# A pre-LN block with linear attention and a gated FFN: a new order for the second half of the loop over k

## The chip, the cores and the metric

One core of a Trainium2 chip runs the whole program. The core has engines that run side by side, each with its own queue of instructions in a fixed order: TensorE (PE, matmuls and the weight loads that go with them), VectorE (DVE), ScalarE (ACT), GpSimd (POOL), and SyncE (SP), which here only issues DMAs. Engines wait for each other by semaphores. The metric is the device time of one execution in microseconds (us), of which the median counts.

## The reference

The input x has 2048 rows of 640. LN is a layer norm without gain.

```python
h  = x + attention(LN(x))
h2 = h + (gelu(LN(h) @ w_gate) * (LN(h) @ w_up)) @ w_down      # 640 -> 1536 -> 640
```

Attention is linear, with 32 heads of 20 columns. q, k and v are x's LN times the three parts of wqkv. With a head's w_phi (20 x 20), the features of q and k are two softmaxes, of q w_phi and of its negative, side by side (40 features). Per head, kv = features(k)^T v (40 x 20) and z = the column sums of features(k) over all rows. The output is features(q) kv / (features(q) z + 1e-6), then a product with wo.

## The kernel before, in words

Rows are split in 16 tiles t of 128, and these in four blocks of 512. All code runs under a schedule written out by hand: after line 663 the kernel is one list of calls such as `vm(12)`, and each engine executes its instructions in the order of that list. Nothing reorders them, so the list is the whole schedule; SP's DMAs stand in it too.

PSUM is cut into four equal buffers, which `gtile` hands out in turn and `give` returns. Every matmul product takes one until another engine has read it out.

The first half of the list loads x and weights, normalises rows and transposes them into LN1T. Per tile t, the loop over k does this:

- `ap(t, e)` normalises the rows on ACT ("a") or DVE ("v"), after `bn`, `rt` and `mr` on DVE and POOL; `dt(t)` transposes them by a DMA from SP into LN1T.
- `vm(t)` (L328) is the product for v, `ve(t)` copies it on ACT into vS. vS has eight buffers, for t modulo 8.
- `fm(i, d)` (L354) multiplies a part of W_q (i = 0) or W_k by the block-diagonal w_phi, `fc` copies it out. So `km(t)` (L375) is the product for k w_phi, and `ke(t, s)` (L382) its exponential on ACT, for s = 0 and its negative for s = 1, into E (eight buffers).
- `ks(t)` (L391) sums E per head on DVE, `kr(t)` (L395) takes the reciprocal into rs (three buffers), `kx(t, s, e)` (L401) multiplies v by it into vt, on DVE ("v") or POOL ("g"). So the softmax's division is put on v.
- `kv(t)` (L416) is called a visit here: 40 small matmuls (32 columns of E against 42 or 63 of vt) that add tile t's k^T v into kvp, which keeps one of the four PSUM buffers from the first visit to the last. The visits may come in any order of t.

`kv_clear` (POOL) builds a mask in parts, and `kv_mask` (DVE, L426 and L429) turns kvp into KV with it, after the last visit.

`qm(j)` (L444) is the product for q w_phi of one or two chunks of 128 columns for a block of 512 rows, `qe(j, s)` (L448) its exponentials on ACT. Then comes attention per tile: `ab` (L489, PE), `ae` (copy out of PSUM), `a_den`, `a_rec`, `a_w`, `a_o` (division and sum, DVE or POOL), a transpose by PE (`o_tr`, `o_tc`) or DMA (`o_dt`), `po_` (L544, the product with W_o), `res` (the residual). LN of h is `ap2` with `tr2` and `tc2`, or `dt2`. The FFN is `gu` (L617, gate and up products for one of 12 chunks of 128 columns), `gl` (gelu, ACT, L623), `gm` (product, DVE, L630) and `dn` (L642, the product with W_down). `gu(0, ...)` is the first FFN block. `gu` asks for all of W_gate and W_up, `po_` for all of W_o.

`load_w(name, c0, c1)` (L171) loads a part of W_o ("o"), W_gate ("g"), W_up ("u") or W_down ("d"). W_down's tile is taken in `ffn_pools()`, in memory that E and vt have used, so its loads wait for the last visit. SP issues its DMAs in order, and one that waits holds up those behind it.

Of the kernel before, what the change touches and what calls it, by code (L numbers as in the profile page):

```python
# [9 lines left out]
F32 = mybir.dt.float32  # L10
# [7 lines left out]
def kernel(  # L18
# [13 lines left out]
    P = 128  # L32
# [62 lines left out]
    def eq_tiles(pool, j0, j1):  # L95
# [9 lines left out]
    epsd = const.tile([P, 1], F32, name="epsd")  # L105
    eq_tiles(const, 0, 13)

    mid = ctx.enter_context(tc.tile_pool(name="mid", bufs=1, side="right"))
    LN1T = [mid.tile([P, NC, 512], BF16, name=f"LN1T{b}") for b in range(NB)]
    Wq2 = mid.tile([P, NC, D], BF16, name="Wq2")  # L110
# [3 lines left out]
    Wk2 = p1.tile([P, NC, D], BF16, name="Wk2")  # L114
    vS = [p1.tile([P, H, VC], BF16, name=f"vS{i}") for i in range(8)]
    WqT = p1.tile([P, NC, D], BF16, name="WqT")
    tsum, tsq, tlog, nrstd, prstd, tmean, trstd = (
        p1.tile([P, 4], F32, name=n) for n in ("tsum", "tsq", "tlog", "nrstd", "prstd", "tmean", "trstd"))
    fp_cm = tc.tile_pool(name="fp", bufs=1, side="right", reuse_waits="tile")
    fp = fp_cm.__enter__()  # L120
    WkT = fp.tile([P, NC, D], BF16, name="WkT")
# [141 lines left out]
    def rt(t, n, e):  # L263
        need(*(("bn", t + j) for j in range(n)))
        m = mv[t][0]
        ve, rstd = small(p1, [P, n], "ve1"), small(p1, [P, n], "rstd1")
        if e == "a":
            nc.scalar.activation(ve, m[:, :, 1], ACTF.Ln, bias=eps)
            nc.scalar.activation(rstd, ve, ACTF.Exp, scale=-0.5)
        else:  # L270
            nc.gpsimd.tensor_scalar_add(ve, m[:, :, 1], EPS)
            nc.gpsimd.tensor_tensor(rstd, ve, nhalf[:, 0:n], op=ALU.pow)
        for j in range(n):
            lnp[t + j] = [m[:, j, 0:1], rstd[:, j:j + 1], None]

    def mr(t):
        mean, rstd, _ = lnp[t]
        lnp[t][2] = small(p1, [P, 1], "mr1")
        nc.gpsimd.tensor_scalar(lnp[t][2], mean, rstd, -1.0, op0=ALU.mult, op1=ALU.mult)
# [42 lines left out]
    def vm(t, c0=0, c1=NC, by_chunk=True):  # L322
        need(*(("lnT", t, c) for c in range(c0, c1)), *(("Wv", c) for c in range(c0, c1)))
        if c0 == 0:
            pv[t] = gtile("pv")
        order = [(c, u) for c in range(c0, c1) for u in range(2)]
        for c, u in order if by_chunk else sorted(order, key=lambda x: x[1]):
            nc.tensor.matmul(pv[t][:, u, 0:HD], lhsT=lnT(t, c), rhs=Wv[:, c, u * HD:(u + 1) * HD],  # L328
                             start=(c == 0), stop=(c == NC - 1))
        if c1 == NC:  # L330
            have.add(("pv", t))

    def ve(t):
        need(("pv", t), *([("prstd", t)] if t in CT else []))
        nc.scalar.activation(vS[t % 8][:, :, 0:Dh].rearrange("p (u h) f -> p u h f", u=2),
                             pv[t][:, :, 0:HD].rearrange("p u (h f) -> p u h f", f=Dh), ACTF.Copy,
                             scale=col(prstd, t) if t in CT else 1.0)
        give(pv.pop(t))
        have.add(("v", t))
# [39 lines left out]
    def ke(t, s):  # L379
        if t not in Ek:  # L380
            Ek[t] = ev.tile([P, 2, D], BF16, name="E", bufs=EB)
        nc.scalar.activation(halves(Ek[t][:, s, :]), pk[t][:, :, 0:HD], ACTF.Exp,  # L382
                             scale=((col(prstd, t), col(nrstd, t)) if t in CT else (1.0, -1.0))[s])
        have.add(("ke", t, s))
        if ("ke", t, 1 - s) in have:
            give(pk.pop(t))

    def ks(t):
        need(("ke", t, 0), ("ke", t, 1))
        sk[t] = small(p1, [P, 2 * H], "sk")  # L390
        nc.vector.reduce_sum(sk[t], Ek[t].rearrange("p s (h f) -> p (s h) f", f=Dh), axis=AX.X)  # L391

    def kr(t):
        rs[t] = small(p1, [P, 2 * H], "rs")
        nc.vector.reciprocal(rs[t], sk.pop(t))  # L395

    def kx(t, s, e):
        need(("v", t))
        if t not in Vt:
            Vt[t] = ev.tile([P, 2, H, VC], BF16, name="vt", bufs=EB)  # L400
        E[e].tensor_tensor(Vt[t][:, s], vS[t % 8], rs[t][:, s * H:(s + 1) * H, None].to_broadcast([P, H, VC]), ALU.mult)  # L401
        have.add(("vt", t, s))
# [3 lines left out]
    def kv(t):  # L406
        need(("vt", t, 0), ("vt", t, 1))
        first, last = not kvn, len(kvn) == NT - 1
        if first:
            kvp.append(gtile("kvp"))  # L410
        kvn.append(t)
        for s in range(2):
            for c in range(NC):
                for g, r in enumerate(QT):
                    f0, h0 = 160 * g + 32 * c, 8 * g + HS[c]
                    nc.tensor.matmul(kvp[0][r, s, HO[c] * VC:(HO[c] + HW[c]) * VC], lhsT=Ek[t][:, s, f0:f0 + 32],  # L416
                                     rhs=Vt[t][:, s, h0:h0 + HW[c], :], start=(c == 0 and first),
                                     stop=last, skip_group_check=True)
        if last:
            have.add("kv")  # L420
# [477 lines left out]
    ap(11, "a")  # L898
    dt(11)
    kr(5)  # L900
    kx(5, 1, "g")
    bn(14, 1, 2)
    rt(14, 2, "g")
    kx(5, 0, "g")
    mr(14)
    kx(4, 0, "v")
    ks(6)
    kr(6)
    kx(6, 0, "g")
    mr(15)  # L910
    kx(6, 1, "v")
    ke(8, 0)
    vm(10, by_chunk=False)
    kv(3)
    ve(10)
    ks(8)
    km(10)
    ke(10, 1)
    fm(0, 0)
    fc(0, 0, "a")  # L920
    ke(10, 0)
    kv(4)
    kv(2)
    km(12)
    ke(12, 0)
    ke(12, 1)
    ks(7)
    ap(1, "v")
    kr(7)
    kx(7, 0, "g")  # L930
    kx(7, 1, "g")
    ks(9)
    kr(9)
    kr(8)
    kx(8, 0, "g")
    ap(2, "v")
    ap(14, "a")
    load_w("o", 0, 2)
    load_w("o", 2, 5)
    dt(14)  # L940
    vm(12, by_chunk=False)
    vm(11, by_chunk=False)
    ve(11)
    ve(12)
    km(13)
    ke(13, 1)
    fm(0, 2)
    fc(0, 2, "a")
    ks(12)
    kr(12)  # L950
    kx(12, 0, "v")
    ks(10)
    kx(9, 0, "g")
    kx(8, 1, "g")
    kx(9, 1, "g")
    kx(12, 1, "g")
    vm(13, by_chunk=False)
    kv(5)
    kv(6)
    kv(7)  # L960
    ke(13, 0)
    ks(13)
    kr(13)
    ve(13)
    ap(15, "a")
    vm(14, by_chunk=False)
    ve(14)
    fm(0, 4)
    fc(0, 4, "a")
    km(14)  # L970
    fm(0, 1)
    fc(0, 1, "a")
    ke(14, 1)
    km(11)
    ke(11, 1)
    ke(14, 0)
    ke(11, 0)
    dt(1)
    dt(2)
    qm(0)  # L980
    qe(0, 1)
    qe(0, 0)
    dt(15)
    vm(15, by_chunk=False)
    ve(15)
    km(15)
    ke(15, 0)
    qm(3)
    qe(3, 1)
    qe(3, 0)  # L990
    ke(15, 1)
    qm(1)
    qe(1, 1)
    qe(1, 0)
    kr(10)
    kx(10, 0, "g")
    kx(13, 0, "g")
    kx(10, 1, "g")
    kv(8)
    kv(10)  # L1000
    kv(12)
    kx(13, 1, "v")
    ks(14)
    kr(14)
    kx(14, 1, "g")
    kv(13)
    ks(11)
    kx(14, 0, "v")
    qm(2)
    qe(2, 1)  # L1010
    qe(2, 0)
    kr(11)
    kx(11, 0, "g")
    kx(11, 1, "g")
    kv(11)
    ks(15)
    kr(15)
    kx(15, 0, "v")
    kx(15, 1, "v")
    kv(14)  # L1020
    kv(9)
    kv(15)
    kv_mask(0)
    ffn_pools()
    qm(4)
    qe(4, 0)
    kv_clear(5)
    kv_clear(6)
    kv_mask(2)
    kv_mask(1)  # L1030
    ab(0)
    ae(0, 1, "v")
    ae(0, 0, "a")
# [1 line left out]
    a_rec(0)  # L1035
    a_w(0, "v")
    a_o(0)
    qe(4, 1)
    qm(5)
    qe(5, 1)  # L1040
    ab(1)
    ae(1, 0, "a")
    ae(1, 1, "a")
    a_den(1, "g")
    a_rec(1)
    a_w(1, "v")
    a_o(1)
    qe(5, 0)
    qm(6)
    o_tr(0)  # L1050
    qe(6, 1)
    o_tc(0, "a")
    qe(6, 0)
    qm(7)
    qe(7, 1)
    po_(0)
    res(0, True)
    o_tr(1)
# [7 lines left out]
    ab(2)  # L1066
    ae(2, 1, "a")
    ae(2, 0, "a")
    a_den(2, "g")
    qm(11)  # L1070
    qe(11, 1)
    qe(11, 0)
    qm(10)
    qe(10, 0)
    ap2(0, "v")
    tr2(0)
    tc2(0, "a")
    qe(10, 1)
    qm(9)
    qe(9, 1)  # L1080
    ap2(1, "v")
    tr2(1)
    a_rec(2)
    tc2(1, "v")
    qe(9, 0)
    qm(12)
    qe(12, 0)
    ab(3)
    ae(3, 0, "a")
    ae(3, 1, "a")  # L1090
    qe(12, 1)
    load_w("g", 0, 1)
    load_w("g", 1, 2)
    load_w("g", 2, 3)
    load_w("g", 3, 4)
    load_w("g", 4, 5)
    load_w("d", 0, 3)
    load_w("d", 3, 6)
    load_w("d", 6, 9)
    load_w("d", 9, 12)  # L1100
    load_w("u", 0, 1)
    load_w("u", 1, 2)
    load_w("u", 2, 3)
    load_w("u", 3, 4)
    load_w("u", 4, 5)
    gu(0, 8, 0, 256)
    gu(0, 2, 0, 256)
    gl(0, 2, 0, 256)
    gu(0, 6, 0, 256)
    gl(0, 6, 0, 256)  # L1110
    a_w(2, "g")
    a_o(2)
    o_dt(2)
    gm(0, 2, 0, 256)
    gl(0, 8, 0, 256)
    gm(0, 8, 0, 256)
    a_den(3, "g")
    gu(0, 3, 0, 256)
    gl(0, 3, 0, 256)
    gm(0, 3, 0, 256)  # L1120
    a_rec(3)
    a_w(3, "g")
    gm(0, 6, 0, 256)
    gu(0, 1, 0, 256)
    gl(0, 1, 0, 256)
    gm(0, 1, 0, 256)
    gu(0, 0, 0, 256)
    a_o(3)
    o_dt(3)
    ab(4)  # L1130
    gl(0, 0, 0, 256)
# [441 lines left out]
```

## Time and profile before

| | us |
|---|---|
| median of 3 runs (275.58 to 276.24) | 275.88 |
| the profiled execution | 276.53 |
| its span, first to last instruction | 274.8 |
| PE busy in the span | 268.1 |
| DVE busy | 176.0 |
| ACT busy | 137.1 |
| POOL busy | 92.8 |

The profile is of one execution. Times in it count from the start of the span. A row of a timeline gives the start, the length, the engine, the line, the operation with what it writes and reads, the count, and in brackets the idle time ahead of it with what ended that. The chain of waits goes back from the last instruction, at each step to what released it. "issue" in it is time in which an engine waited for nothing that the profile shows. SPq is SP's queue; its rows are the issuing of DMAs, and the landing comes later. Some matmul records are missing from a trace, so that a count can be one or two short. PE's granted clock is at full speed throughout.

### The profile page before, as it was taken

To read this page: it belongs to the slowest core of one execution; us is meant where nothing else is said; L and a number is where in the kernel's file an instruction comes from. 1 tells how busy PE (TensorE), PEld (TensorE's weight loads), DVE (VectorE), ACT (ScalarE), POOL (GpSimd) and SP (SyncE) were. 2 spreads that over 40 slices of the span, in tenths; PEclk is the share of its full clock that TensorE was granted. 3 is DMA by queue.
4 is the path that set the end of the run, shared out by engine and by line. 5 is a ranking of instruction groups with operands and counts; after the bars stand their busy time and mean duration, and the time that the engine had idled before them with its cause. 6 is when DMAs were issued, how large, how long until landed. Compare 5 with 4: busy or idle time off the path is not lost.

```text
span 274.8 us, 7125 instructions
## 1 busy us (share of the span) xinstructions
PE 268.1 (98%) x2966; PEld 171.1 (62%) x2981; DVE 176.0 (64%) x328; ACT 137.1 (50%) x238; POOL 92.8 (34%) x215
## 2 busy tenths in 40 slices
PE   8999998999899999999999999999999999999995
PEld 4777776765455887788754544765554576444574
DVE  6799999987477587577377955985367413143413
ACT  5968996796699864273615333421305340222200
POOL 4678998997003013441500230330100140000000
PEclk9999999999999999999999999999999999999999
DMA  7963779580590131321123012075001713000002
GB/s 210 184 234 74 114 105 170 99 286 3 190 379 10 26 26 29 72 44 31 40 38 95 3 29 43 2 119 54 0 0 48 122 35 100 10 0 1 24 2 95
DMA packets 43392, 21.62 MB, mean 79 GB/s; under 512 B 35936, under 2 KB 41312, under 8 KB 43360
## 3 DMA queue, kind: packets, MB, share of 16 engines
q1 hardware_dynamic: 43360, 21.17, 33.9%
q8 instruction: 23, 0.38, 0.6%
q14 instruction: 9, 0.07, 0.1%
HBM read 10.18 MB, written 2.62 MB: 47 GB/s over the span
## 4 chain that ended last, share of the span: by engine, by line
PE 96%; DMA 2%; issue 1%; DVE 0%; ACT 0%
PE gu L617 38%; PE pd L642 19%; PE po L544 8%; PE pq L444 8%; PE pv L328 8%; PE pk L375 7%; PE ab L489 2%; PE kvp L416 2%; DMA LN1T<-ln 2%; PE wu L311 1%; PE tp L148 1%; PE wa L354 1%; PE wu L315 0%; ACT E L382 0%; DVE y L652 0%
## 5 line engine op out<-in xcount | busy, mean ns | idle before, releaser
L630 DVE TENSOR_TENSOR GT<-gu,g 128x512 bf16<-128x512 f32 (+1 forms) x60 | 34.0, 581 | 48.7 <-ACT g L623 48.4
L623 ACT ACTIVATE g<-gu 128x512 bf16<-128x512 f32 (+1 forms) x60 | 29.7, 511 | 70.7 <-PE gu L617 70.5
L617 PE MATMUL gu<-LN2T,Wg 128*128 128x512 bf16 (+1 forms) x291 | 61.3, 335 | 0.5
L617 PE MATMUL gu<-LN2T,Wu 128*128 128x512 bf16 (+1 forms) x300 | 61.7, 336 | 0.0
L642 PE MATMUL pd<-Wd,GT 128*128 128x320 bf16 (+2 forms) x396 | 54.0, 295 | 0.0
L642 PEld LDWEIGHTS <-GT 128*128 128x128 bf16 x396 | 37.6, 98 | 14.3 <-DVE GT L630 0.3
L617 PEld LDWEIGHTS <-Wu 128*128 128x128 bf16 x300 | 29.4, 98 | 22.6
L617 PEld LDWEIGHTS <-Wg 128*128 128x128 bf16 x300 | 29.0, 98 | 21.7
L401 POOL TENSOR_TENSOR vt<-vS,rs 128x672 bf16<-128x672 bf16 x24 | 33.4, 1413 | 2.4 <-DVE rs L395 1.8
L652 DVE TENSOR_TENSOR y<-pd,x_sb 128x640 bf16<-128x640 f32 (+3 forms) x18 | 13.1, 744 | 23.6 <-PE pd L642 23.6
L328 PE MATMUL pv<-Wv,LN1T 128*128 128x320 bf16 x160 | 24.2, 299 | 1.1 <-DMA LN1T<-ln 1.0
L522 DVE TENSOR_TENSOR tt<-AB,w 128x1280 bf16<-128x1280 f32 x16 | 23.8, 1490 | 0.9 <-POOL w L516 0.6
L544 PE MATMUL po<-Wo,oT 128*128 128x320 bf16 x160 | 24.2, 299 | 0.0
L391 DVE TENSOR_REDUCE sk<-E 128x64 f32<-128x1280 bf16 x16 | 23.1, 1463 | 1.6 <-ACT E L382 1.6
L375 PE MATMUL pk<-Wk,LN1T 128*128 128x320 bf16 x160 | 23.5, 299 | 0.0
L444 PE MATMUL pq<-LN1T,Wq 128*128 128x512 bf16 x94 | 22.9, 379 | 0.4 <-issue 0.2
L448 ACT ACTIVATE Eq<-pq 128x1024 bf16<-128x1024 f32 (+1 forms) x26 | 20.4, 848 | 5.6 <-PE pq L444 5.6
L578 POOL TENSOR_SCALAR v<-sm 128x1 f32<-128x1 f32 x14 | 4.9, 351 | 53.4 <-DVE x_sb L565 51.5
L128 ACT COPY AB<-ab 128x704 f32<-128x704 f32 x20 | 14.2, 744 | 11.7 <-DVE tt L522 9.7
L328 PEld LDWEIGHTS <-LN1T 128*128 128x128 bf16 x160 | 15.1, 98 | 7.8 <-DMA LN1T<-ln 1.3
L544 PEld LDWEIGHTS <-oT 128*128 128x128 bf16 x160 | 15.5, 98 | 6.8 <-ACT oT L128 0.4
L382 ACT ACTIVATE E<-pk 128x640 bf16<-128x640 f32 x26 | 17.8, 712 | 3.7 <-PE pk L375 3.3
(103 smaller groups left out, 285.3 us busy)
## 6 DMA issues: line engine op xcount, KB each, us to landing
out_dram<-y SPq DMA_DIRECT2D x15, 160.0 KB, 1.9
x_sb<-in_A_x_dram SPq DMA_DIRECT2D x6, 320.0 KB, 4.9
Wg<-in_B_w_gate_dram SPq DMA_DIRECT2D x5, 384.0 KB, 5.8
Wd<-in_B_w_down_dram SPq DMA_DIRECT2D x4, 480.0 KB, 5.7
Wu<-in_B_w_up_dram SPq DMA_DIRECT2D x5, 384.0 KB, 8.6
x_sb<-in_A_x_dram SPq DMA_DIRECT2D x4, 160.0 KB, 3.2
Wv<-in_A_wqkv_dram SPq DMA_DIRECT2D x2, 320.0 KB, 4.2
Wo<-in_A_wo_dram SPq DMA_DIRECT2D x1, 480.0 KB, 5.0
```

The lines of the kernel that those rows point to most:

```text
L328: nc.tensor.matmul(pv[t][:, u, 0:HD], lhsT=lnT(t, c), rhs=Wv[:, c, u * HD:(u + 1) * HD], start=(c == 0), stop=(c == NC - 1))
L375: nc.tensor.matmul(pk[t][:, u, 0:HD], lhsT=lnT(t, c), rhs=Wk2[:, c, u * HD:(u + 1) * HD], start=(c == 0), stop=(c == NC - 1))
L391: nc.vector.reduce_sum(sk[t], Ek[t].rearrange("p s (h f) -> p (s h) f", f=Dh), axis=AX.X)
L401: E[e].tensor_tensor(Vt[t][:, s], vS[t % 8], rs[t][:, s * H:(s + 1) * H, None].to_broadcast([P, H, VC]), ALU.mult)
L444: nc.tensor.matmul(pqs[j][:, i, :], lhsT=Wq2[:, kc, c * P:(c + 1) * P], rhs=LN1T[b][:, kc, :], start=(kc == 0), stop=(kc == NC - 1))
L448: nc.scalar.activation(Eq[j][:, :, s, :], pqs[j][:, 0:len(QG[j])], ACTF.Exp, scale=(1.0, -1.0)[s])
L522: nc.vector.tensor_tensor(tt.rearrange("p s (h f) -> p s h f", f=Dh), num, w[t][:, :, :, None].to_broadcast([P, 2, H, Dh]), ALU.mult)
L544: nc.tensor.matmul(po[t][:, u, 0:HD], lhsT=oT[t][:, c, :], rhs=Wo[:, c, u * HD:(u + 1) * HD], start=(c == 0), stop=(c == NC - 1))
L617: nc.tensor.matmul(p[:, i, 0:a1 - a0], lhsT=W[:, c, f * P:(f + 1) * P], rhs=LN2T[b][:, c, a0:a1], start=(c == 0), stop=(c == NC - 1))
L623: nc.scalar.activation(x[:, 0:a1 - a0], p[:, 0, 0:a1 - a0], ACTF.Gelu_apprx_tanh)
L630: nc.vector.tensor_tensor(GT[b, f][:, a0:a1], p[:, 1, 0:a1 - a0], x[:, 0:a1 - a0], ALU.mult)
L642: nc.tensor.matmul(pd[k][:, u, n0:n1], lhsT=GT[b, f][:, tl * P:(tl + 1) * P], rhs=Wd[:, f, u * HD + n0:u * HD + n1], start=(f == 0), stop= ...
```

## The change

The list is the same up to `kr(5)`, in the middle of the loop over k, and from the middle of the first FFN block on. Between them the same work stands in another order. These are its parts:

- Visits: before, the groups that follow each other on PE were kv 3; 4, 2; 5, 6, 7; 8, 10, 12, 13; 11, 14, 9, 15. Now they are 3, 2; 4, 5; 8, 6; 12, 13, 7; 11, 9, 14, 10, 15.
- The products for v and k come in another order of tiles (10, 12, 13, 14, 11, 15 for v; 10, 13, 12, 11, 14, 15 for k), and so do the W_phi products and, on ACT, the copies and exponentials.
- Of the 23 `kx` calls after that point, eight run on DVE where seven did, and fifteen on POOL where sixteen did.
- Loads: before, both parts of W_o were issued ahead of `dt(14)`, and all of W_gate, W_down and W_up after the first FFN's pools. Now W_o's first part, one part of W_up and one of W_gate come ahead of `dt(15)`, `dt(2)`, `dt(1)`; the rest of W_gate and one more part of W_up follow these; W_o's second part stands behind two parts of W_down and one of W_up after the visits, and the rest comes last.
- Between the visits and the first FFN block, `a_den(1)`, `o_tc(0)` and half of `ae(3)` go to DVE, `a_w(1)` to POOL and `a_w(2)` to DVE, `qm(9)`, `qm(10)` and `qm(11)` change places, and `gu(0, 2)` comes ahead of `ab(3)`.
- Two small tiles (`tmean`, `trstd`) move to another pool. That adds two lines, so that line numbers behind it are higher by two.

```diff
     kr(5)
-    kx(5, 1, "g")
     bn(14, 1, 2)
-    rt(14, 2, "g")
-    kx(5, 0, "g")
-    mr(14)
-    kx(4, 0, "v")
     ks(6)
     kr(6)
+    kx(6, 1, "v")
+    kx(5, 0, "g")
+    rt(14, 2, "g")
+    mr(14)
+    kx(5, 1, "g")
+    kx(4, 0, "g")
+    mr(15)
     kx(6, 0, "g")
-    mr(15)
-    kx(6, 1, "v")
     ke(8, 0)
     vm(10, by_chunk=False)
+    km(10)
+    fm(0, 4)
     kv(3)
+    kv(2)
     ve(10)
...
-    load_w("o", 0, 2)
-    load_w("o", 2, 5)
     dt(14)
...
+    load_w("o", 0, 2)
     fm(0, 2)
+    ke(14, 0)
+    ke(14, 1)
     fc(0, 2, "a")
+    load_w("u", 0, 1)
+    load_w("g", 1, 2)
+    dt(15)
...
+    dt(2)
+    dt(1)
+    qm(0)
+    qe(0, 1)
+    ke(15, 1)
+    qm(1)
+    ke(15, 0)
...
+    load_w("g", 4, 5)
+    load_w("g", 0, 1)
+    load_w("g", 2, 3)
+    load_w("u", 1, 2)
+    load_w("g", 3, 4)
...
+    kv(11)
+    kv(9)
+    kx(14, 1, "v")
+    kv(14)
+    kv(10)
+    kv_clear(5)
     kx(15, 1, "v")
-    kv(14)
-    kv(9)
     kv(15)
     kv_mask(0)
+    kv_mask(1)
+    kv_mask(2)
+    kv_clear(6)
+    qm(4)
+    qe(4, 1)
     ffn_pools()
...
+    load_w("d", 3, 6)
+    load_w("u", 2, 3)
+    load_w("d", 6, 9)
     ab(0)
...
+    a_w(1, "g")
+    a_o(1)
+    load_w("o", 2, 5)
     po_(0)
...
     load_w("d", 0, 3)
-    load_w("d", 3, 6)
-    load_w("d", 6, 9)
     load_w("d", 9, 12)
-    load_w("u", 0, 1)
-    load_w("u", 1, 2)
-    load_w("u", 2, 3)
     load_w("u", 3, 4)
     load_w("u", 4, 5)
+    gu(0, 2, 0, 256)
+    ab(3)
+    ae(3, 1, "a")
+    ae(3, 0, "v")
```

## The prediction

> **What bounds the kernel now.** I read the page first, then the chain of waits, then the timelines of PE, DVE and the DMA queue between 36 and 98 us. From the page:
>
> ```profile
> PE 268.1 (98%) x2966; PEld 171.1 (62%) x2981; DVE 176.0 (64%) x328; ACT 137.1 (50%) x238; POOL 92.8 (34%) x215
> q8 instruction: 23, 0.38, 0.6%
> PE 96%; DMA 2%; issue 1%; DVE 0%; ACT 0%
> ```
>
> PE is the bound. The change issues the same matmuls, so it can only win back holes in PE's stream, or make new ones. The chain shows where the holes between 39 and 76 us are (start, length, what):
>
> ```profile
> 40.97 0.34 ACT E L382
> 41.31 4.50 DMA LN1T<-ln
> ...
> 68.27 0.48 PE kvp L416 x47
> 68.74 0.36 issue
> 69.11 1.07 PE kvp L416 x97
> ...
> 72.45 0.16 PE ab L489 x5
> 72.60 0.22 issue
> 72.82 0.43 PE ab L489 x25
> ```
>
> PE's timeline gives each hole its price, by the starts of the groups:
>
> ```profile
> 43.32 1.52 PE L328 MATMUL pv<-Wv,LN1T 128*128 128x320 bf16 x10
> 45.85 1.53 PE L328 MATMUL pv<-Wv,LN1T 128*128 128x320 bf16 x10 [1.01 <-DMA LN1T<-ln]
> 47.22 1.52 PE L375 MATMUL pk<-Wk,LN1T 128*128 128x320 bf16 x10
> ...
> 64.53 1.47 PE L416 MATMUL kvp<-vt,E 128*32 128x42 bf16 x160
> 65.94 2.33 PE L444 MATMUL pq<-LN1T,Wq 128*128 128x512 bf16 x9
> 68.20 0.55 PE L416 MATMUL kvp<-vt,E 128*32 128x42 bf16 x48
> 69.11 1.07 PE L416 MATMUL kvp<-vt,E 128*32 128x42 bf16 x112 [0.36 <-issue]
> ```
>
> vm(12) to vm(11) is 2.53 us start to start where ten such matmuls take 1.37: 1.16 lost. Four k^T v visits take 1.41 at 64.53; the four at 68.20 last until PE's next group at 70.34, of which one matmul is missing from the records (x9, 0.22), so 1.92: about 0.5 lost. From 73 to 97 us the chain is PE without a hole; nothing can be won there.
>
> Why vm(11) waited is in the DMA queue:
>
> ```profile
> 40.00 2.54 SPq L301 DMA_TRANSPOSE LN1T<-ln  x2
> 42.59 2.08 SPq L171 DMA_DIRECT2D Wo<-in_A_wo_dram  x2
> 70.30 2.56 SPq L171 DMA_DIRECT2D Wd<-in_B_w_down_dram  x4
> ```
>
> The second transpose, issued at 41.31, is dt(11); W_o's 800 KB are issued right behind it and it lands after 4.50 us, against a median of 2.6 for this kind.
>
> **Part by part.** The profiled run took 276.53 us (span 274.8), 0.65 above the median of 275.88. I sum against it and carry the difference over. I follow each queue from 37.55, where km(8) ends in the last stretch that both have in common. Durations: vm or km 1.36, a W_phi product 0.32, qm of two chunks 2.16, a k^T v visit 0.35 to 0.4 plus 0.2 for each group of visits (both ways), an exponential or copy on ACT 0.60 to 0.65, LN apply on ACT 0.8, a sum on DVE 1.47, reciprocal 0.5, vt 0.86 on DVE, 1.32 on POOL (1.9 beside one on DVE).
>
> *vm(11)'s wait goes.* dt(11) no longer has W_o behind it, and vm(11) and km(11) come later. First user is km(11): vm(10), km(10), fm, two visits, fm, vm(12), vm(13), km(13), two visits and km(12) come ahead, 10.6 us, so PE is there at 48.1, against a landing at 43.9 (2.6) to 45.8 (4.50). What comes sooner instead: vm(12) at 41.7 (dt(12), issued 38.68, takes 2.7: 41.4) and vm(13) at 43.1 (dt(13), issued 40.00, 42.6). Margins of 0.3 and 0.5: nothing added. Gain 1.16.
>
> *PSUM slots.* kvp keeps one of four, so each product waits for ACT to empty another. ACT after ap(11) ends at 39.16: ke(8,0), ve(10), fc, two exponentials, fc, ap(14) run to 44.1; ve(13) starts when vm(13) is done (44.6). The closest are vm(12), vm(13) and km(14), with 0.2 to 0.35 us to spare; the others have 0.5 and more. ke(14) must also wait for kv(8), whose E buffer it takes: 54.3 against vm(15)'s need of that slot at 56.3 leaves 0.7. Cost 0, up to 0.4 if these slip. No gain is possible.
>
> *The visits.* DVE from 38.5 to vt(15,1): ten sums 14.7, ten reciprocals 5.0, eight vt 6.9, two LN 0.9, bn 0.6: ends at 66.6. It is one vt more than before, but in the old order DVE waited twice for ACT's exponentials (0.74 and 0.91) because ke(15,1) stood behind qm(3)'s and others; now ke(15,0) ends at 62.1 and sums start there. POOL: vt(9,1) waits for its reciprocal until 50.4 (a vt's reciprocal comes from DVE, and each reciprocal waits for one of three rs buffers that an earlier vt must have read; along this order none of these comes last but the 50.4), then ten vt with three beside DVE's, 14.8, to 65.2, and the mask's last part and copy, 3.5 (65.97 to 69.5 before), to 68.7. PE's own work from 37.55 to the end of the visits is twelve vm and km 16.3, four fm 1.3, fourteen visits 5.0 in five groups 1.0, seven chunks of qm 7.6: 31.2, to 68.7; the old end of 70.1 less 1.66 gives 68.5. So kv(15) starts at about 68.2 and ends at 68.6. kv(15) has 1.5 us to spare; the mask on DVE has qm(4)'s 2.16 as cover before ab(0) needs it at 70.9. Cost 0; if DVE's late vt each take the 1.56 that one at 61.26 took, DVE ends 2.8 later and PE loses 1.3.
>
> *The hole of 0.5 in the visits.* From the restart at 69.11 to that at 72.82 there are 112 + 10 + 5 = 127 matmuls, with their weight loads 254 instructions, and the page's instruction queue brought 23 pieces for 5,947 recorded PE instructions, 259 each. So I take both holes as waits for the next piece: one cannot be crossed sooner than 3.7 us after the last. Counted off in the new order, the same boundaries lie 15 matmuls into kv(7), 8 into kv(14) and 5 into ab(0). kv(7) to kv(14) now holds qm(3), qm(2) and two visits: 4.5 us, no hole. kv(14) to ab(0) is 3.4: the hole of 0.3 at ab(0) stays. Gain 0.5, from 0 (holes of another cause) to 0.8 (both go). The Trainium skill (Runtime: NRT & Kernel Launch, section Instruction fetch mechanics) has blocks of 16 KiB or 256 instructions, which the 254 bear out, but calls the fetch hidden by the dispatch rate, which 0.36 and 0.22 us of issue do not. By that sentence both holes would be of another cause and the sum 0.5 smaller.
>
> *Loads.* W_o's first part, one of W_up, one of W_gate (1.09 MB) go ahead of dt(15), dt(2), dt(1). dt(15) is issued at 48.1, dt(2) at 50.1, dt(1) at 51.4. At 2.6 to 4.50 us they land by 52.6, 54.6, 55.9; km(15) needs the first at 54.9, qm(0) the rest at 57.6. Cost 0, hidden by km(14), two visits and the k and v products of 15. The other W_gate loads have until gu, at 88. After the visits the queue holds W_down, W_up, W_down, then W_o's second part (1.82 MB to its end), which po_(0) needs. Before, four W_down loads (1.92 MB) issued from 70.30 had landed 9.3 us later (issue at 72.38, 7.2). From 68.7 that is 77.9 at the latest, and po_(0) is due at 79.0. Cost 0, margin 1.1.
>
> *Attention to gu.* a_den(1) moves to DVE and a_w(1) to POOL, o_tc(0) and ae(3,0) to DVE, qm(9) to qm(11) and gu(0,2) change places. From ab(0)'s end (71.5): o(0) takes 1.1 + 3.3 as before, to 75.9, PE's transpose is due at 76.4. o(1): 75.9 + 0.5 + 0.4 + wait for AB(1) 0.3 + o_tc(0) 0.5 + tt and o 2.0 = 79.7; due at 80.3. po_(1), ab(2), qm(10) and qm(12) have 0.1 to 0.4 over ACT's exponentials, much as before. Cost 0, up to 0.6.
>
> Sum: 276.53 - 1.16 - 0.5 = 274.87, for the median 275.88 - 1.66 = **274.2**. Beyond gu(0,0) the order is the old one, PE-bound throughout.
>
> **Rivals.** *W_o is late.* po_(0) holds up PE, its queue is in order. For it: the wait is new, and the next loads share the engines, as with dt(11) (4.50 instead of 2.6). If all eight end together, by the old queue (last W_up issued 74.86, 9.6 later: 14.1 us for 3.84 MB) 3.55 MB land after 13.0, at 81.7: PE waits 2.7, the net is +1.0, 276.9. It decides from 80.7, 12 us after the visits. Against: the old loads landed in order, 3.9 to 7.2 us after issue for the first four.
>
> *Margins eaten.* Several of the small ones slip, or DVE's vt run late (POOL's 0.90 for a mask step of 0.18 at 66.44, beside DVE's vt, speaks for it): 0.7 to 1.4 come back, 274.9 to 275.6. A stall in PE's stream needs one late input only, and some twenty inputs stand within 1 us. The Trainium skill (SBUF — State Buffer, section SBUF: two separate sides) has a DVE and a GpSimd instruction exclude each other from a shared pair of ports for their whole length; the 0.90 agrees with it.
>
> *Holes not from fetching*: 275.88 - 1.16 = 274.7, within the first case's range.
>
> *Transposes late.* dt(1) behind 1.09 MB lands after 57.6: against it, 1.7 us of margin at the slowest transpose seen.
>
> **Numbers.** Forecast 0.66 (273.4 to 274.9: both holes gone and ab(0)'s too, down to only vm(11)'s), margins eaten 0.15 (a third of it within 0.2%, which is about what a measurement can tell), W_o late 0.12, transposes or something else unseen 0.07, 0.04 slower and 0.03 no change. Faster by over 0.2% (below 275.33): 0.66 + 0.10 of the eaten margins = 0.76. Slower (above 276.43): 0.12 + 0.04 = 0.16. Same: 0.05 + 0.03 = 0.08. Range 273.4 to 276.3: it leaves out the late W_o in its full size.
>
> **What would show it.** Right: no wait for LN1T at PE's L330, which is this line's new number; five visits in one group without an issue hole; an issue hole of some 0.2 to 0.4 in ab(0) still there; kvp's end near 68.6; gu from 88.3 rather than 90.4. Wrong: PE waiting for a DMA of Wo at po, for vt in the visits, or for ACT in the products from 41 us on; then the gain shrinks by that wait.

## The result, and the profile after

The changed kernel takes 274.81 us (median of 8 runs, 274.36 to 275.10). The kernel before took 275.53 on the same chip (8 runs, 275.13 to 276.24). The ratio is 0.9973, with a 95% interval of 0.9961 to 0.9985, so the gain is 0.72 us (0.4 to 1.1). The profiled execution took 274.87 with a span of 273.2. Against the profiled execution of before (276.53, 274.8) that is 1.66 less, more than twice the gain of the medians. Further down, each run stands against the kernel before timed beside it, on one of two chips; the ratios given are not the quotients of the two medians and can differ from them by 0.001. Most of what follows is about that difference, and about what made dt(11) late.

From the page of the changed kernel, the three lines that answer to those shown of before:

```profile
PE 268.7 (98%) x2981; PEld 171.0 (63%) x2981; DVE 178.1 (65%) x333; ACT 135.6 (50%) x236; POOL 89.3 (33%) x212
q8 instruction: 23, 0.38, 0.6%
PE 95%; DMA 2%; SPq 1%; DVE 1%; issue 0%
```

PE works as long as before (268.1 then) and is still the bound; the instructions come in 23 pieces as before. PE's timeline of the changed kernel (start, length, line, operation, count, idle time ahead in brackets):

```profile
46.90 2.89 PE L377 MATMUL pk<-Wk,LN1T 128*128 128x320 bf16 x20
49.63 2.88 PE L330 MATMUL pv<-Wv,LN1T 128*128 128x320 bf16 x20
...
66.74 1.81 PE L418 MATMUL kvp<-vt,E 128*32 128x42 bf16 x200
68.48 2.33 PE L446 MATMUL pq<-LN1T,Wq 128*128 128x512 bf16 x10
70.74 0.23 PE L491 MATMUL ab<-KV,Eq 32*128 32x44 bf16 x5
71.18 0.43 PE L491 MATMUL ab<-KV,Eq 32*128 32x66 bf16 x35 [0.22 <-issue]
...
88.27 0.71 PE L619 MATMUL gu<-LN2T,Wg 128*128 128x256 bf16 x5
```

The twenty matmuls at 46.90 are km(12) and km(11), the first to need dt(11); those at 49.63 are vm(14) and vm(11). None of them pauses: the wait for LN1T is gone. The five last visits (200 matmuls) run in 1.74 us without a pause. The pause inside ab(0) is there, as forecast: from 70.74 to the next group at 71.55 are 0.81 us, where ab(0) without a pause takes 0.40. From there the chain of waits is PE alone until past the start of the FFN at 88.27. SP's queue in the changed kernel, and the transposes issued at 40.1 and 41.4, dt(13) and dt(11), with their times to landing:

```profile
38.79 6.83 SPq L303 DMA_TRANSPOSE LN1T<-ln  x4
45.67 0.57 SPq L173 DMA_DIRECT2D Wo<-in_A_wo_dram  x1
```

```profile
L303 SPq DMA_TRANSPOSE LN1T<-ln x2: 1222/1229/1236, 40.1 to 41.4; - x2
DMA to landing us min/median/max: 2.6/3.5/4.4
```

dt(11) is the third of the four transposes, issued at 41.43, and it landed 4.42 us later, as late as before (4.50). But now no load of W_o is issued beside it; the first comes at 45.67. So the change took away the one who waited, not the lateness, which puts the prediction's reason for the lateness in doubt.

### The profile page after: what moved, and what is told of

The parts are those of the page before. It is cut to its first block, busy times and chain, and to the rows that moved or that the text cites. A ratio compares the mean times of both kernels' runs of the same rounds, so it can differ in the third digit from the quotient of the medians.

```text
span 273.2 us, 7140 instructions
## 1 busy us (share of the span) xinstructions
PE 268.7 (98%) x2981; PEld 171.0 (63%) x2981; DVE 178.1 (65%) x333; ACT 135.6 (50%) x236; POOL 89.3 (33%) x212
## 4 chain that ended last, share of the span: by engine, by line
PE 95%; DMA 2%; SPq 1%; DVE 1%; issue 0%
PE gu L619 38%; PE pd L644 19%; PE pq L446 8%; PE po L546 8%; PE pk L377 8%; PE pv L330 7%; PE ab L491 2%; PE kvp L418 2%; DMA x_sb<-in_A_x_dram 2%; PE wa L356 1%; PE tp L150 1%; SPq L156 0%; DVE stats L260 0%; SPq L160 0%; DVE LN1T L130 0%
## 5 line engine op out<-in xcount | busy, mean ns | idle before, releaser
L403 POOL TENSOR_TENSOR vt<-vS,rs 128x672 bf16<-128x672 bf16 x23 | 30.3, 1344 | 4.3 <-DVE rs L397 4.0
L546 PEld LDWEIGHTS <-oT 128*128 128x128 bf16 x160 | 15.5, 98 | 6.9 <-ACT oT L130 0.2
L130 ACT COPY AB<-ab 128x704 f32<-128x704 f32 x19 | 13.6, 743 | 12.4 <-DVE tt L524 9.8
```

What stands on the lines that cost most here:

```text
L546: nc.tensor.matmul(po[t][:, u, 0:HD], lhsT=oT[t][:, c, :], rhs=Wo[:, c, u * HD:(u + 1) * HD], start=(c == 0), stop=(c == NC - 1))
```

## The experiments

Two theories of dt(11) were set against each other: W_o's loads make it late (the prediction's), or the fetch of a piece of PE's instructions does. In both profiles such a 16 KB packet of the instruction queue runs while dt(11) is in flight (42.85 to 44.27 before, 42.74 to 44.36 after). This is the DMA view of the kernel before from 42 to 45 us, cut in 40 slices of 0.075 us. The first line has what the DMA engines moved in each slice; the line of the instruction queue has packets, MB and share of time, and the last line ends with the landing time:

```profile
GB/s 89 14 0 0 0 0 14 99 181 195 229 406 215 191 215 137 51 14 0 0 0 0 0 0 0 0 0 0 0 0 10 7 7 10 10 7 10 10 10 10
q8 instruction: 1, 0.02, 3.0%
LN1T<-ln SPq DMA_TRANSPOSE x1, 4.5
```

dt(11)'s packets flow from 42.45 on. The fetch starts in the slice with 406 (its 16 KB are counted there). Half a us later no packet starts any more, for 0.9 us (twelve slices of 0), and the trickle begins again at 44.25, when the fetch ends.

**The kernel before, once more.** No edit.

> The kernel before, unchanged, to see how far two profiles of it differ. Its first profile (276.53 us) had 1.16 us lost ahead of vm(11) and 0.5 in the last visits, which the changed kernel's profile (274.87) does not have: 1.66 between the two profiles, while the medians of eight runs differ by 0.72 (275.53 and 274.81). If the holes are the same in each execution, this profile shows 1.1 to 1.2 and 0.4 to 0.6 again and the 0.9 must come from elsewhere (the start). If the holes vary, one of them is smaller here. Timed against itself: a ratio of 1.000 within 0.002.

It took 275.63 (10 runs) against 275.54 (29 runs): ratio 1.0, 0.9983 to 1.0017. The profiled execution took 275.62. Its PE timeline:

```profile
43.63 1.52 PE L328 MATMUL pv<-Wv,LN1T 128*128 128x320 bf16 x10
45.40 1.53 PE L328 MATMUL pv<-Wv,LN1T 128*128 128x320 bf16 x10 [0.25 <-DMA LN1T<-ln]
...
67.72 1.55 PE L416 MATMUL kvp<-vt,E 128*32 128x42 bf16 x160
69.43 2.11 PE L444 MATMUL pq<-LN1T,Wq 128*128 128x512 bf16 x9 [0.16 <-issue]
71.47 0.22 PE L489 MATMUL ab<-KV,Eq 32*128 32x44 bf16 x5
71.91 0.43 PE L489 MATMUL ab<-KV,Eq 32*128 32x66 bf16 x35 [0.22 <-issue]
```

The same program has other holes. From vm(12) to vm(11) are 1.77 us, so 0.40 lost instead of 1.16: dt(11) took 4.21 and landed 0.46 earlier than in the first profile, and PE came 0.31 later. The four last visits lose 1.71 less one missing matmul of 0.22 less 1.41, which is 0.08 instead of 0.5. ab(0)'s pause is the same. So the first profile was an unfavourable execution, and its holes are not those of the median.

**Only W_o's loads moved.**

```diff
-    load_w("o", 0, 2)
-    load_w("o", 2, 5)
     dt(14)
...
     dt(15)
+    load_w("o", 0, 2)
+    load_w("o", 2, 5)
```

> The kernel before with W_o's two loads moved from ahead of dt(14) to behind dt(15), nothing else. The predicted theory (W_o's 800 KB behind dt(11) make it land after 4.5 us instead of 2.6): dt(11) lands at about 43.9, the wait ahead of vm(11) goes, 0.7 to 1.2 us faster. Rival, from the changed kernel's trace, where dt(11) took 4.4 us with no load near it: a fetch of PE instructions (16 KB, at 42.85 before, 42.74 after) stops the transposes for about 2 us; then dt(11) lands after 4.4 to 4.5 as before, the wait stays, and the time is the same within 0.2 us.

275.62 against 275.54: ratio 0.9991, 0.9978 to 1.0004, no difference that can be measured. SP's queue, the transposes dt(13) and dt(11) with their times to landing, and PE's timeline:

```profile
38.92 14.91 SPq L301 DMA_TRANSPOSE LN1T<-ln  x7
53.87 1.08 SPq L171 DMA_DIRECT2D Wo<-in_A_wo_dram  x2
```

```profile
L301 SPq DMA_TRANSPOSE LN1T<-ln x2: 1222/1224/1227, 40.2 to 41.5; - x2
DMA to landing us min/median/max: 2.6/3.5/4.5
```

```profile
43.69 1.52 PE L328 MATMUL pv<-Wv,LN1T 128*128 128x320 bf16 x10
46.05 1.53 PE L328 MATMUL pv<-Wv,LN1T 128*128 128x320 bf16 x10 [0.83 <-DMA LN1T<-ln]
```

Nothing but transposes is issued until 53.87, and dt(11) still takes 4.45 us (41.55 to 46.00) and vm(11) still waits: 2.36 less 1.37 is 0.99. So W_o's loads do not make dt(11) late. The fetch, at 42.85 to 44.51, is where it was.

**Only the waiting product moved.** In the kernel before, km(13) ahead of vm(11), so that vm(11) comes 1.36 us later.

```diff
     vm(12, by_chunk=False)
+    km(13)
     vm(11, by_chunk=False)
     ve(11)
     ve(12)
-    km(13)
```

> The kernel before with km(13) ahead of vm(11) instead of behind ve(12): one call moved, the loads and visits as before. vm(11) then asks for its transpose 1.36 us later, at 46.0. If the wait ahead of vm(11) is all that this spot costs, its hole goes from 1.16 to under 0.1 in the profile and the time falls by as much as the hole is worth in an undisturbed run: 1.1 by the first profile, 0.2 to 0.6 if the smaller difference of the medians (0.72) says that the hole is often smaller. Either theory of its cause gives the same here.

276.37 against 275.54: ratio 1.0021, 1.0008 to 1.0033, slower, where a gain was expected. PE's timeline:

```profile
44.95 1.52 PE L375 MATMUL pk<-Wk,LN1T 128*128 128x320 bf16 x10
46.30 1.52 PE L328 MATMUL pv<-Wv,LN1T 128*128 128x320 bf16 x10
48.62 0.47 PE L354 MATMUL wa<-BD,WqT 128*128 128x140 bf16 x6 [0.79 <-ACT vS L335]
49.21 1.52 PE L328 MATMUL pv<-Wv,LN1T 128*128 128x320 bf16 x10
```

The wait for LN1T is gone and another has come: fm(0,2) needs the PSUM buffer that ACT's ve gives back, and loses 0.96, with 0.27 more at the next product. One product moved alone carries its wait to the next PSUM buffer. The changed kernel has no such wait; it also reordered the W_phi products and ACT's copies, which is the likely reason, though no run tests that alone.

**Eight visits in a row.** In the changed kernel, qm(3) and qm(2) are put ahead of the last eight visits, so that one piece of 256 instructions lies in visits alone.

```diff
+    qm(3)
+    qe(3, 1)
+    qe(3, 0)
+    qm(2)
+    qe(2, 0)
+    qe(2, 1)
     kv(12)
...
     ks(15)
-    qm(3)
-    qe(3, 1)
-    qe(3, 0)
-    qm(2)
-    qe(2, 0)
-    qe(2, 1)
```

> The changed kernel with qm(3) and qm(2) ahead of kv(12), so that eight visits (640 PE instructions in 2.9 us) follow each other. Fetch theory: boundaries of 256 instructions lie at the end of kv(13) (66.5), 8 matmuls into kv(14) and 5 into ab(0); one cannot be crossed sooner than 3.7 us after the last, so kv(14) stops from 67.6 to 70.2: a hole of 2.5, and again about 0.3 at ab(0); 2.4 to 2.6 us slower than the changed kernel, 277.3 or 1.7 slower than before. Rival (the hole of before was a late vt or the mask, not fetching): all inputs are there as in the changed kernel, hole under 0.3, time within 0.3 us of the changed kernel's.

278.41 (4 runs), 1.0098 times before (1.0077 to 1.012), and 3.60 above the changed kernel. PE's timeline, and then stretches of the same run (stretch, its length, busy time and count of each engine, PE's granted clock, DMA share, GB/s):

```profile
66.49 1.88 PE L418 MATMUL kvp<-vt,E 128*32 128x42 bf16 x207
70.37 1.07 PE L418 MATMUL kvp<-vt,E 128*32 128x63 bf16 x113 [2.00 <-issue]
71.38 0.55 PE L446 MATMUL pq<-LN1T,Wq 128*128 128x512 bf16 x1
72.15 3.25 PE L446 MATMUL pq<-LN1T,Wq 128*128 128x512 bf16 x8 [0.22 <-issue]
75.33 0.47 PE L491 MATMUL ab<-KV,Eq 32*128 32x44 bf16 x40
```

```profile
71.00:72.00 1.00, 0.93 (x56) 0.60 (x45) 0.36 (x2) 0.00 (x0) 0.00 (x0) 0.74 0.09 16
72.00:73.00 1.00, 0.85 (x2) 0.29 (x2) 0.57 (x2) 0.00 (x0) 0.00 (x0) 0.50 0.40 31
73.00:74.00 1.00, 1.00 (x4) 0.43 (x3) 0.00 (x0) 0.00 (x0) 0.00 (x0) 0.50 0.66 180
74.00:75.00 1.00, 1.00 (x4) 0.30 (x3) 0.00 (x0) 0.00 (x0) 0.00 (x0) 0.56 0.99 332
75.00:76.00 1.00, 1.00 (x43) 0.53 (x43) 0.09 (x1) 0.57 (x1) 0.00 (x0) 1.00 0.75 139
```

The hole of 2.0 us (2.5 expected) is where the count of instructions put it: after 207 matmuls, 7 into the sixth visit, kv(14), where 8 were expected. A fetch runs in that hole, at 68.05 to 69.16; PE goes on 1.2 us after that. This bears out that a piece can't be crossed faster than its successor comes in. The hole of 0.3 expected at ab(0) did not come (0.40 from 75.33 to the next group at 75.73). The rest was not forecast: about 1 us after the hole PE's granted clock falls to 0.50, by the rows from 71 to 75 for 0.52 + 1 + 1 + 0.88 = 3.4 us, and qm(4), 2.26 us in the changed kernel, takes 3.95. 2.0 and 1.7 make 3.7, about the 3.6 between the medians. All four executions have a mean clock of 0.994 (0.999 to 1.0 in those of the changed kernel), so this is not one execution's accident. The Trainium skill (TensorE: Matmul & The Clock Gate, section What's actually happening) has the clock fall back after an idle window of some 3.4 us that runs freely; here 2.0 us without a matmul, between visits of small ones, were enough.

**Every fetch moved.** The kernel before with 128 small matmuls more. They shift the pieces by 134 instructions from the start to vm(13), and by 256, a whole piece and so back to the same places, behind it.

```diff
+    def tiny(p, n, a):
+        for i in range(n):
+            nc.tensor.matmul(p[QT[i % 4], 0, 0:42], lhsT=a[:, 0:32], rhs=a[:, 0:42], start=True, stop=True)
...
         if c0 == 0:
             pv[t] = gtile("pv")
+        if t == 13:
+            tiny(pv[t], 61, Wv[:, 0])
...
-    warm(1, 1)
-    warm(1, 2)
-    warm(1, 3)
+    tiny(wu, 70, zero)
```

> The kernel before with 128 small matmuls more (42 columns, overwritten by what follows): 70 in place of three warm-up matmuls, which moves every later piece of TensorE's instructions by 134 places, and 61 at the head of vm(13), which moves the pieces behind it back to where they were. The k^T v visits and everything behind them lie in their pieces as before. Fetch theory (a transpose is stopped while the 16 KB of a piece come in): the piece that came in at 42.8 to 44.3, in dt(11)'s flight, now comes at about 46 to 47; the one before it moves to about 39.0 to 40.5, where dt(12) or dt(13) is in flight. So dt(11) lands 2.6 to 3.0 after its issue instead of 4.2 to 4.5, dt(12) or dt(13) takes 3.2 to 4.5 instead, which their products can bear (vm(12) is due 4.6 after dt(12)'s issue), and the hole ahead of vm(11) is 0 to 0.1. Time: 275.6 less the hole of 0.4 to 1.1 plus 0.6 for the 61 matmuls, 275.1 to 275.8. Rival, that dt(11) is late for its place among the other loads and transposes: it takes 4.2 to 4.5 again, the hole stays, and the 61 matmuls are added: 276.2.

276.43 (12 runs) against 275.31: ratio 1.0038, 1.0017 to 1.0059, slower, and outside both figures. The time alone speaks rather for the rival; the profile doesn't. PE's timeline:

```profile
11.02 0.44 PE L148 MATMUL tp<-ident,ln 128*128 128x128 bf16 x5
12.38 0.80 PE L360 MATMUL wa<-BD,WkT 128*128 128x140 bf16 x12 [0.92 <-POOL kmask L190]
...
43.25 1.53 PE L381 MATMUL pk<-Wk,LN1T 128*128 128x320 bf16 x10
44.62 2.88 PE L334 MATMUL pv<-Wv,LN1T 128*128 128x320 bf16 x20
...
49.10 0.64 PE L319 MATMUL pv<-Wv 128*32 128x42 bf16 x61
```

vm(12) and vm(11) (x20 at 44.62) run without a hole, but that proves nothing: PE comes to vm(11) at 45.98 here, 1.3 us later than before, and a dt(11) that took 4.2 to 4.5 would have landed by 45.85. Only the landing times can tell. What is lost lies elsewhere: 0.58 for the small matmuls at 49.10 up to the next group at 49.68, and some 1.1 at 11.3 to 12.4, ahead of the first W_phi product. The row names POOL, but WkT is what came last. Its second transpose landed at 12.33, 5.77 us after its issue, where the kernel before had 3.96 and 4.36 in its two profiles, and the six other runs 3.99 to 4.88. A fetch that the two profiles of before have at 15.5 runs here at 8.32 to 10.40, over these transposes of W_k. So the shift helped one transpose and made others late.

The fetch in the loop came at 42.07 to 43.03 and the next at 47.81 to 48.75, both later than expected, as PE itself was over 1 us late while SP issued as before. The second transpose of the three (dt(13)) answers to it. The transposes that were issued at 38.7 and 40.0 (dt(12) and dt(13)), with their times to landing:

```profile
L301 SPq DMA_TRANSPOSE LN1T<-ln x2: 1222/1222/1222, 38.7 to 40.0; - x2
DMA to landing us min/median/max: 2.7/3.4/4.1
```

dt(13) took 4.14 instead of 2.6, dt(11) behind it 3.38 instead of 4.2 to 4.5 (2.6 to 3.0 expected: missed, the fetch was still in its flight), and dt(14), met by the fetch at 47.81, took 3.44 instead of 2.60. The late ones moved with the fetch.

**W_o's loads put back.** The changed kernel with both of W_o's loads ahead of dt(14).

```diff
+    load_w("o", 0, 2)
+    load_w("o", 2, 5)
     dt(14)
...
-    load_w("o", 0, 2)
...
-    load_w("o", 2, 5)
     po_(0)
```

> The changed kernel with both of W_o's loads put back ahead of dt(14). Fetch theory: W_o's place does not touch the transposes; the late ones are those with a fetch in their flight, dt(14) stays at 2.6 to 3.1 if none comes then. po_(0), which had 0.07 us to spare on W_o's second part, has over 10. Time 274.8 within 0.4, or 0.1 to 0.4 below the changed kernel if po_(0) has waited in some of its executions. W_o theory of the prediction: dt(14), with W_o's 800 KB issued right beside it, takes 4.2 to 4.5 and delays vm(14): 275.2 to 275.8.

274.76 (12 runs) against 275.31: ratio 0.9973, 0.9956 to 0.9989, the changed kernel's own. But dt(14) did become late. SP's queue, dt(14)'s time to landing, and PE:

```profile
42.97 2.27 SPq L173 DMA_DIRECT2D Wo<-in_A_wo_dram  x2
45.34 1.20 SPq L303 DMA_TRANSPOSE LN1T<-ln  x1
```

```profile
DMA to landing us min/median/max: 4.6/4.6/4.6
```

```profile
47.20 2.89 PE L377 MATMUL pk<-Wk,LN1T 128*128 128x320 bf16 x20
49.97 2.89 PE L330 MATMUL pv<-Wv,LN1T 128*128 128x320 bf16 x20
```

No fetch ran from 44.35 to 51.23, and dt(14) took 4.58 where the changed kernel has 2.58: W_o's loads, the last issued 0.56 us ahead of it and landing at 47.71 and 49.26, are what the edit put there. vm(14) started 0.05 us after its landing, just as PE came free, so it cost next to nothing. The expectation's fetch theory alone (2.6 to 3.1) was too narrow: here dt(14) took about what the theory of W_o's loads gave it (4.2 to 4.5), so loads just ahead of a transpose can make it late too. They need not: in the kernel before the same loads were issued 3.6 us and more ahead of dt(14), the second was in flight until 48.20, and dt(14), issued at 46.86, took 2.60. dt(11) in the kernel before had no load ahead of it.

**The changed kernel, once more.** No edit.

> The changed kernel once more, unchanged. If its gain is from the two holes that it has no more, its profile repeats: no wait ahead of vm(11), no issue hole in the last five visits, one of 0.2 in ab(0) again, dt(11) late again (4.2 to 4.5) with no one waiting for it; 274.8 within 0.3. If W_o's second part is a close call at po_(0), a wait of 0 to 0.5 for it is to be seen there.

274.58 (12 runs) against 275.31: ratio 0.9968, 0.9951 to 0.9986. The profiled execution took 274.18:

```profile
66.39 1.81 PE L418 MATMUL kvp<-vt,E 128*32 128x42 bf16 x200
68.12 2.33 PE L446 MATMUL pq<-LN1T,Wq 128*128 128x512 bf16 x10
70.39 0.54 PE L491 MATMUL ab<-KV,Eq 32*128 32x44 bf16 x40
```

dt(11) took 4.38 again and nobody waited. The visits have no hole. ab(0) lost 0.07 only, where 0.2 was expected: that hole, too, comes and goes. W_o's second part landed at 77.19, 0.94 ahead of po_(0).

The holes of the profiled executions, worked out from starts as above, in us:

| kernel | time | ahead of vm(11) | last visits | ab(0) |
|---|---|---|---|---|
| before | 276.53 | 1.16 | 0.5 | 0.40 |
| before, again | 275.62 | 0.40 | 0.08 | 0.40 |
| before, W_o's loads moved | 275.83 | 0.99 | 0 | 0.08 |
| changed | 274.87 | 0 | 0 | 0.41 |
| changed, again | 274.18 | 0 | 0 | 0.07 |
| changed, W_o's loads back | 274.81 | 0 | 0 | 0 |

The three of before lose 0.85 on average ahead of vm(11) and 0.2 in the visits. That is 1.05 that the change can win back, at the upper end of the 0.4 to 1.1 that the timed runs give it; the first of the three executions lies 1.0 above the median of its kernel. Three executions are too few to say more.

The place of the hole in the visits is fixed where its size is not. Five profiles keep the four last visits of before: behind the 48th of their 160 matmuls, 8 into kv(14), the next one comes late by 0.55, 0.11, 0 (W_o's loads moved), 0.18 (vm(11) moved) and 0.32 (fetches moved). It is the place that the prediction took for a boundary.

A third hole is in neither the table nor the prediction. The three visits that start at 50.35 in the first profile take 1.26, and 1.24 to 1.26 in all five profiles with that order, where three visits of the changed kernel take 1.07 (at 62.33). So 0.2 more went with the new order; its cause is open. In the two first profiles it is offset: the changed kernel was 0.20 later at the end of km(8), where the new order begins. So their difference of 1.66 matches the forecast's gain by coincidence.

No version here is measurably faster than the changed kernel.

## Why the prediction was right, and where it was not

*vm(11)'s wait goes.* Right that it goes, and this is the larger part of the gain. Two things failed. The cause, "W_o's 800 KB are issued right behind it", fell with the run that moved only these loads (4.45 without them). In its place stands the fetch of PE's instructions, shown by the landing times in the run that moved the fetches (4.14 and 3.44 where 2.6 was usual) and by the counts at the end of this document. And the term of 1.16 was one execution's: other profiles of the same work have 0.40 and 0.99.

*The hole of 0.5 in the visits.* The mechanism was right. Where the count of instructions was made to bite, it gave 2.0 us. Its size was not: 0.5 in one execution, 0.08 and 0 in two others. The two terms together were 1.66 by the one profile, and 1.05 by three, while the timed runs give 0.72. So the gain was forecast more than twice too large. The measured 274.81 lies inside the range, and inside the likeliest case's 273.4 to 274.9, but this owes something to luck: the forecast started from the median of three runs, 275.88, where eight give 275.53. The start 0.35 too high hid a part of the gain that was 0.94 too large, and 274.2 came out 0.6 low. From 275.53, even 1.05 would give 274.5. The text had compared the profiled time to the median (0.65 above) and carried the difference over as if it had nothing to do with the holes; by the second profile of before, at 275.62, holes are a part of it. One price was also too high: each group of visits was charged 0.2 beside its matmuls, and the changed kernel's groups of two, three and five take 0.76, 1.07 and 1.74, some 0.35 a visit and under 0.1 a group. The 0.2 fits only the group with the third hole.

*ab(0)'s hole stays.* Right in the first profile (0.41), but 0.07 and 0 in two others.

*PSUM slots, at no cost.* Right: no wait for ACT in the products of the changed kernel. That it isn't so of itself shows in the run that moved vm(11) alone, which lost 0.96 and 0.27 to them.

*The visits' inputs, at no cost.* Right: DVE's last vt ended at 67.17 (66.6 forecast), which left kv(15) 1.0 and not 1.5, and the mask at 68.60 (68.7). qm(4) starts at 68.48, where the last visits were put at 68.6. Single vt on DVE took 1.98, as the rival of eaten margins had it, but kv(15) had the room.

*Loads.* Right in the result, thin in one number. W_o's second part, issued at 70.75, landed 8.00 us later at 78.75, where 77.9 was forecast; po_(0) started at 78.82. The margin was 0.07 and not 1.1, and 0.94 in the second profile. The run with W_o's loads back, landed 29 us before po_(0), is as fast, so this cost nothing in the median. dt(15) took 5.06 and landed at 53.43, past the 52.6 of the forecast's bound (loads ahead of it and a fetch at 50.93 to 51.89), and km(15) had room.

*Attention to gu.* Right: gu starts at 88.27, 88.3 forecast.

*The rivals.* W_o late did not decide, by 0.07 us in one profile. Margins eaten gave 274.9 to 275.6, close to what came, but its mechanism is absent: no late input stops PE in the changed kernel. Holes not from fetching gave 274.7, the nearest figure, for the wrong reason: the run with eight visits in a row shows that the hole in the visits is from fetching. ab(0)'s hole, at another such boundary by the count, was not tested alone. By the Trainium skill (Runtime: NRT & Kernel Launch, section Instruction fetch mechanics) the fetch is hidden by the dispatch rate; the 2.0 us of issue in that run say that with matmuls of 9 ns it is not.

## What to carry to other kernels

A hole that one profile shows is one draw: before a gain is sized by it, look at a second profile of the same kernel, and do not carry a profile's excess over the median past the sum. Where a product waits for a DMA, look at everything that ran beside that DMA, the instruction queue too, before naming the load next to it. And a wait is not won by moving the one that waits: the PSUM buffer behind it must come free earlier too, or the wait moves there.

## What the runs showed of the hardware that was not expected

A transpose by DMA that is in flight when a 16 KB piece of PE's instructions comes in (0.9 to 2.1 us long) lands late. In the nine profiles, of the transposes of normalised rows and of o (LN1T, LN2T and oT; 2.6 us as a rule), 52 of 64 took over 3.6 us where such a fetch ran at some time between 1.0 and 2.2 us after the issue, and 9 of 297 elsewhere. Where the fetch started 1.0 to 1.5 us after the issue it was 30 of 30; where none ran between issue and landing it was 1 of 229, dt(14) in the run with W_o's loads back. What in the DMA engines makes them stop isn't shown.

With matmuls of 9 ns, 256 instructions pass in 1.1 us, and PE stands still for up to 2.0 us until the next piece is in. After the hole of 2.0 us it ran at half its clock for 3.4 us, which made qm(4) 1.7 us longer. How little work brings the clock down was not measured.
